# Top-k attention and two feed-forward blocks: a planner that begins score blocks and value blocks later than their inputs allow

## The chip, the cores and the metric

One core of a Trainium2 chip runs the whole program. The metric is the device time of one execution in microseconds (us); the kernel before takes 1037.14 us (median of 3 runs, 1036.56 to 1039.12). The engines are named as in the profile: PE (TensorE, matmuls; PEld its weight loads), DVE (VectorE), ACT (ScalarE), POOL (GpSimd) and SP, which issues the DMAs. Each engine works through a list of its own, one instruction after the other, and waits on semaphores for the others.

## The reference

Three stages, with 4 batches, 8 heads, 576 positions and head size 64, so 2304 rows of 512 values:

```python
scores = scale * np.matmul(q, k.transpose(0, 1, 3, 2))
kth = np.partition(scores, -top_k, axis=-1)[..., -top_k:-top_k + 1]   # top_k = 32
scores = np.where(scores >= kth, scores, -1000000000.0)
attn = np.exp(scores - np.max(scores, axis=-1, keepdims=True))
attn = attn / (np.sum(attn, axis=-1, keepdims=True) + 1e-09)
x = np.matmul(attn, v)                       # to 2304 x 512
h = x @ w_in
x = np.where(h > 0.0, h, np.exp(np.minimum(h, 0.0)) - 1.0) @ w_out
out = ((x @ w1) * (x @ w2)) @ w3 @ w_out2    # w_in 512x2048, w1 and w2 512x1024
```

## The kernel before, in words

**Tiles.** The 2304 rows are cut into 9 chunks of 256 rows, numbered 0 to 8. A chunk's attention is 8 tiles: 4 pairs of heads times 2 blocks of 128 rows. Its feed-forward part (function `mlp`) follows when the last tile is done. Most products are made from a high and a low half in 16 bits, so one product is three matmuls.

**One tile of attention**, in the order of its data:

- *Score block* (L529, PE): 4 matmuls `psS<-kt,qh` and `psS<-kt,ql` for one of the two heads. There is one `psS`, so the next score block can only start when ACT has copied this one into `s` (L531).
- *Top-k* (DVE): per head four MAX8 (L539) and three MATCH_REPLACE8 (L541) over 576 scores, in `wk`.
- *Weights*: ACT makes the mask and the exponential (L554, L556) and the high half (L564), POOL the low half (L565), and SP issues one transposing DMA per head, `pt<-pi` (L567).
- *Value block* (L582, PE): 28 matmuls `psA<-vv,pt`. There is one `psA` too; ACT reads the denominators from it (L593), DVE inverts and scales (L596, L599), ACT and POOL split the result (L602, L603), and SP issues `x<-xt` (L604), which makes a part of the chunk's `x`.

**The feed-forward part of a chunk** on PE: 16 A blocks (L841 to L843, `psR<-x,win`), 16 O blocks (L878 to L880, `psY<-g,wout`), two small gram products on the result (Y: L898, L903), 16 B blocks (L920 to L922, `psR<-x,w`), 12 matmuls each, and 8 D blocks (L955 to L957) of 6. A blocks read `x` of all eight tiles. Between A and O stand ACT and POOL (L853 to L865), in Y DVE (L891, L902, L904), between B and D ACT, DVE and POOL (L930 to L946).

**The weights** come as 64-bit numbers and are turned into scaled 16-bit halves in the first 250 us (L633 to L679, L783), while the first chunks' attention already runs.

**What sets the order.** No scheduler of the language: `Program.op` records every piece of work with an engine, an assumed cost, its inputs and outputs and a rank. `emit` then plans a timetable by list scheduling (`forward`, `backward`, then `forward` again, `fb=2` times): an operation becomes ready when its inputs have ended, plus an assumed latency (table `LAT`, times `slack` between engines), and an engine takes the ready one with the best rank. The instructions are written in the order of the planned starts. So a planned time decides only the order; on the chip nothing waits for it, only for semaphores. The table `OFF` (some 240 numbers, one for each group of work and engine) shifts the ranks of the first pass.

Of the kernel before, what the change touches and what calls it, by code (L numbers as in the profile page):

```python
# [32 lines left out]
PAR = dict(rings=(2, 3, 4, 3, 1, 2, 5, 3), nxs=3, nxf=2, nxt=3, slack=1.6, fb=2, snake=1, blag=0, hv={}, lv={'wi': 16, 'wo': 16}, whole=(), cd={'wi': [0, 0, 6], 'wo': [0, 0, 6], 'w34': [0, 0, 8], 'w12': [8, 0, 8]}, pv=-577.81, pi=702.591, p34=-453.754, po=123.714, p12=822.408,   # L33
# [5 lines left out]
OFF = {":DVE": 16163, "A0:ACT": -38685, "A0:DVE": -4543, "A0:PE": 21441, "A0:POOL": 23849, "A1:ACT": 1589, "A1:PE": -13628, "A1:POOL": -11110,  # L39
# [35 lines left out]
       "att8x:SP": 2116, "attsa:ACT": -38945, "attsa:PE": -45630, "attsk:ACT": -46655, "attsk:POOL": -12175, "attsk:SP": -20106, "attsm:ACT": 59355,  # L75
       "attsm:POOL": 27934, "attsp:ACT": -27773, "attsp:POOL": 4475, "attsp:SP": 12804, "attsq:ACT": -29254, "attsq:POOL": 26261, "attsq:SP": -8330,
       "attss:ACT": -10714, "attss:PE": -9165, "attst:DVE": 53351, "attsv:ACT": 18840, "attsv:DVE": 15311, "attsv:SP": 12330, "attsx:ACT": 11365,
# [3 lines left out]
       -8612, "w_in.c:ACT": 800, "w_in.c:DVE": 9028, "w_in.c:PE": -11799, "w_in.c:POOL": -7583, "w_in.n:DVE": 24888, "w_in.n:PE": 9694, "w_in:ACT":  # L81
       -220, "w_in:DVE": -7426, "w_in:POOL": -33659, "w_in:SP": -55119, "w_out.c:ACT": 5219, "w_out.c:DVE": -531, "w_out.c:PE": -22400,
       "w_out.c:POOL": -5233, "w_out.n:DVE": -38749, "w_out.n:PE": 8892, "w_out:ACT": 14086, "w_out:DVE": 35892, "w_out:POOL": 23776, "w_out:SP":
       23054, "w_v0:DVE": -70692, "w_v0:PE": -2179, "w_v0:SP": -19017, "w_v1:DVE": -12335, "w_v1:PE": 38647, "w_v1:SP": 59851, "w_v:DVE": -36828}


# [17 lines left out]
class Program:  # L104
# [30 lines left out]
    def forward(self, succ, rank):  # L135
# [6 lines left out]
        rt = [0.0] * n  # L142
# [949 lines left out]
```

## Time and profile before

| what | us |
|---|---|
| median of 3 runs | 1037.14 |
| the profiled execution, its own time | 1037.07 |
| its span, first to last instruction | 1035.3 |
| PE busy | 955.4 (92%) |
| DVE busy | 870.8 (84%) |
| ACT busy | 819.4 (79%) |
| POOL busy | 739.7 (71%) |

A page of the profile has a sum for each engine, which hides when it was busy. The stretches have to be read apart: in some of them one engine is full, and only work on that engine's list, or a wait in it, moves the end. Times in the profile count from the start of the span.

### The profile page before, as it was taken

The numbers are of one execution on the slowest core, as the hardware profiler recorded it, in microseconds if no ns is written. First come the engines' busy times: TensorE is split into PE (matmuls) and PEld (weight loads), VectorE is DVE, ScalarE is ACT, GpSimd is POOL, SyncE is SP. The second block draws the span as 40 slices with busy tenths as digits, with TensorE's granted clock in tenths as the row PEclk, the third lists the DMA queues.
The fourth block names the chain that finished last, engine by engine and source line by source line (L and its number), as shares of the span: only waits on it lengthen the run. The fifth ranks groups of instructions, "written<-read, shape, count | busy, mean of one in ns | idle before, by whom it ended". The sixth has DMA issues, their size and how long they took to land.

```text
span 1035.3 us, 24518 instructions
## 1 busy us (share of the span) xinstructions
PE 955.4 (92%) x9096; PEld 770.4 (74%) x9096; DVE 870.8 (84%) x1941; ACT 819.4 (79%) x1517; POOL 739.7 (71%) x795
## 2 busy tenths in 40 slices
PE   2466999896899999999999999999999999999998
PEld 2333455796788878878878897788789889878875
DVE  6999999999999999997999999575999999951010
ACT  6999977998999977976987798587778878944512
POOL 6999966799999846965985597479368657944701
PEclk9897999999999999999999999999999999999999
DMA  9987995867456774555476354524553353330000
GB/s 366 329 273 232 276 251 122 232 197 154 135 126 160 169 137 86 121 136 148 127 175 155 86 121 116 146 57 136 124 132 69 70 114 82 57 91 14 1 22 21
DMA packets 246744, 144.04 MB, mean 139 GB/s; under 512 B 195680, under 2 KB 222304, under 8 KB 246624
## 3 DMA queue, kind: packets, MB, share of 16 engines
q1 hardware_dynamic: 246624, 142.48, 54.1%
q8 instruction: 71, 1.16, 0.5%
q14 instruction: 49, 0.40, 0.1%
HBM read 80.65 MB, written 14.59 MB: 92 GB/s over the span
## 4 chain that ended last, share of the span: by engine, by line
DVE 36%; PE 26%; ACT 15%; POOL 7%; issue 7%; DMA 6%; DVEq 0%; POOLq 0%; ACTq 0%
DVE m L539 16%; DVE wk L541 14%; PE psY L783 3%; PE psR L920 2%; PE psR L921 2%; PE psR L922 2%; DMA pt<-pi 2%; PE psS L529 2%; DMA pp<-w 2%; PE psA L582 2%; ACT s L554 1%; PE psR L841 1%; PE psR L842 1%; PE psR L843 1%; ACT s L531 1%
## 5 line engine op out<-in xcount | busy, mean ns | idle before, releaser
L539 DVE MAX8 m<-wk 128x8 f32<-128x576 f32 x432 | 312.2, 747 | 0.8
L565 POOL TENSOR_TENSOR pi<-s,pi 128x576 f16<-128x576 f32 x144 | 185.5, 1296 | 78.8 <-ACT pi L564 67.7
L541 DVE MATCH_REPLACE8 wk<-m,wk 128x576 f32<-128x576 f32 x288 | 212.5, 741 | 0.0
L920 PE MATMUL psR<-x,w 128*128 128x256 f16 x576 | 157.3, 273 | 3.7 <-DVE t L940 3.7
L841 PE MATMUL psR<-x,win 128*128 128x256 f16 x576 | 157.8, 274 | 0.8 <-DVE t L940 0.5
L843 PE MATMUL psR<-x,win 128*128 128x256 f16 x576 | 157.4, 273 | 0.0
L842 PE MATMUL psR<-x,win 128*128 128x256 f16 x576 | 157.4, 273 | 0.0
L922 PE MATMUL psR<-x,w 128*128 128x256 f16 x576 | 157.0, 273 | 0.5 <-POOL w L670 0.5
L878 PE MATMUL psY<-g,wout 128*128 128x256 f16 x576 | 157.3, 273 | 0.0
L880 PE MATMUL psY<-g,wout 128*128 128x256 f16 x576 | 157.0, 273 | 0.0
L879 PE MATMUL psY<-g,wout 128*128 128x256 f16 x576 | 157.0, 273 | 0.0
L921 PE MATMUL psR<-x,w 128*128 128x256 f16 x576 | 157.0, 273 | 0.0
L554 ACT ACTIVATE s<-s,m 128x576 f32<-128x576 f32 x144 | 110.3, 776 | 40.8 <-DVE m L539 39.2
L529 PE MATMUL psS<-kt,qh 128*128 128x288 f32 x320 | 112.4, 366 | 31.4 <-ACT s L531 24.9
L531 ACT ACTIVATE s<-psS 128x576 f32<-128x576 f32 (+1 forms) x160 | 103.1, 644 | 17.0 <-PE psS L529 11.2
L556 ACT ACTIVATE s<-s,ty 128x576 f32<-128x576 f32 x144 | 107.4, 771 | 3.8 <-POOL ty L550 3.7
L539 DVE MAX8 m<-s 128x8 f32<-128x576 f32 x144 | 106.1, 746 | 3.9 <-ACT s L531 3.4
L541 DVE MATCH_REPLACE8 wk<-m,s 128x576 f32<-128x576 f32 x144 | 106.3, 741 | 0.0
L564 ACT ACTIVATE pi<-s 128x576 f16<-128x576 f32 x144 | 96.5, 679 | 9.4 <-DMA pt<-pi 9.1
L529 PEld LDWEIGHTS psS<-kt,qh 128*128 128x128 f32 x320 | 62.3, 195 | 44.9 <-ACT s L531 20.0
L529 PE MATMUL psS<-kt,ql 128*128 128x288 f32 x320 | 91.5, 300 | 1.0 <-POOL ql L511 1.0
L582 PEld LDWEIGHTS <-pt 128*128 128x128 f16 (+1 forms) x2240 | 77.8, 101 | 17.7 <-issue 8.0
(168 smaller groups left out, 2393.4 us busy)
## 6 DMA issues: line engine op xcount, KB each, us to landing
qr<-qd SPq DMA_DIRECT2D x72, 128.0 KB, 2.7
raw<-kd SPq DMA_DIRECT2D x32, 288.0 KB, 3.3
w<-w_in SPq DMA_DIRECT2D x16, 512.0 KB, 7.5
w<-w_out SPq DMA_DIRECT2D x16, 512.0 KB, 6.0
w<-w3t SPq DMA_DIRECT2D x16, 512.0 KB, 4.8
kd<-kt SPq DMA_DIRECT2D x12, 576.0 KB, 4.0
kt<-kd SPq DMA_DIRECT2D x12, 576.0 KB, 3.9
w<-w SPq DMA_DIRECT2D x12, 512.0 KB, 4.7
```

Source lines behind the costliest of these rows:

```text
L529: T.matmul(psS[:, half, 0:288], lhsT=L[qs][:, hh], rhs=KT[kk][:, hh, half * 288:half * 288 + 288], start=li == 0, stop=li == 1)
L539: op("DVE", 665, lambda r=r, src=src, m8=m8, hh=hh: V.max(m8[:, hh, 8 * r:8 * r + 8], src), [skey], [mk], p1 + PAR["ot"] * STEP)
L541: op("DVE", 727, lambda r=r, src=src, w=w, m8=m8, hh=hh: V.match_replace(w, m8[:, hh, 8 * r:8 * r + 8], src, -3.0e38), [skey, mk], [k], p1 ...
L565: op("POOL", 1240, lambda Y=Y, PIs=PIs, hh=hh: G.tensor_tensor(PIs[:, hh, S:2 * S], Y[:, hh], PIs[:, hh, 0:S], op=OP.subtract), hks, [pk], ...
L841: T.matmul(o, lhsT=hi(W)[:, cs], rhs=X[:, 0, kd_, 0:N], start=kd_ == 0, stop=False)
L842: T.matmul(o, lhsT=hi(W)[:, cs], rhs=X[:, 1, kd_, 0:N], start=False, stop=False)
L843: T.matmul(o, lhsT=lo(W)[:, cs], rhs=X[:, 0, kd_, 0:N], start=False, stop=kd_ == 3)
L878: T.matmul(o, lhsT=hi(W)[:, cs], rhs=rh, start=ft == 0 and m % 2 == 0, stop=False, skip_group_check=True)
L879: T.matmul(o, lhsT=hi(W)[:, cs], rhs=rl, start=False, stop=False, skip_group_check=True)
L920: T.matmul(o, lhsT=hi(W)[:, cs], rhs=X[:, 0, kd_, 0:N], start=kd_ == 0, stop=False)
L921: T.matmul(o, lhsT=hi(W)[:, cs], rhs=X[:, 1, kd_, 0:N], start=False, stop=False)
L922: T.matmul(o, lhsT=lo(W)[:, cs], rhs=X[:, 0, kd_, 0:N], start=False, stop=kd_ == 3)
```

## The change

`Program.op` takes one more argument, `late`; `forward` adds it to the time at which an operation becomes ready. The score blocks and the value blocks get 700 ns, nothing else does. The table `OFF` has new numbers in all its entries (one line of each side stands here for it). Every recorded operation, its inputs and its outputs are the same.

```diff
-PAR = dict(rings=(2, 3, 4, 3, 1, 2, 5, 3), ...
+PAR = dict(wq=700.0, wa=700.0, rings=(2, 3, 4, 3, 1, 2, 5, 3), ...
-OFF = {":DVE": 16163, "A0:ACT": -38685, "A0:DVE": -4543, "A0:PE": 21441, ...
+OFF = {":DVE": 14772, "A0:ACT": -36506, "A0:DVE": -3954, "A0:PE": 23705, ...
...
-    def op(self, eng, cost, fn, r=(), w=(), pr=0.0, lat=None, lk=False):
+    def op(self, eng, cost, fn, r=(), w=(), pr=0.0, lat=None, lk=False, late=0.0):
         i = len(self.ops)
+        if late:
+            self.late[i] = late
...
             for s in succ[i]:
-                rt[s] = max(rt[s], end + (0.0 if e == "SP" else LAT.get(...) * ...))
+                rt[s] = max(rt[s], end + (0.0 if e == "SP" else LAT.get(...) * ...) + self.late.get(s, 0.0))
...
-                        op("PE", 540, qk, [("qh", qs), ("ql", qs), ("k", kk)], ["psS"], pqk)
+                        op("PE", 540, qk, [("qh", qs), ("ql", qs), ("k", kk)], ["psS"], pqk, late=PAR["wq"])
...
-                    op("PE", 930, av, [("v", vs), ("vl", vs), ("pt", pt, 0), ("pt", pt, 1)], [pak], p5)
+                    op("PE", 930, av, [("v", vs), ("vl", vs), ("pt", pt, 0), ("pt", pt, 1)], [pak], p5, late=PAR["wa"])
```

Lines of the changed kernel are numbered 3 higher than those of before (L582 is L585, L593 is L596, and so on).

The lists move everywhere by a few places. Three places matter for what follows.

PE, chunk 6, the last value block (`pt1`, 64 columns: this tile's rows belong to two batches), the score blocks behind it, the next value block (`pt0`) and the chunk's first A block (`x0,win`). Before:

```order
L582 MATMUL psA_153<-vv3_115,pt1_123 64x64
L920 LDWEIGHTS w12_99
...
L529 MATMUL psS_152<-kt2_111,qh0_105 128x288
...
L920 MATMUL psR0_156<-x2_126,w12_99 128x256
...
L529 MATMUL psS_152<-kt2_111,qh1_106 128x288
...
L582 MATMUL psA_153<-vv3_115,pt0_122 128x65
...
L841 MATMUL psR1_157<-x0_124,win_97 128x256
```

After, the same stretch of PE's list:

```order
L585 MATMUL psA_153<-vv3_115,pt1_123 64x64
L532 MATMUL psS_152<-kt2_111,qh0_105 128x288
L532 MATMUL psS_152<-kt2_111,ql0_107 128x288
...
L532 MATMUL psS_152<-kt2_111,qh1_106 128x288
L532 MATMUL psS_152<-kt2_111,ql1_108 128x288
...
L585 MATMUL psA_153<-vv3_115,pt0_122 128x65
...
L844 MATMUL psR1_157<-x0_124,win_97 128x256
```

Before, six B blocks (L920 to L922) stand between that value block and the A block, two ahead of each of three score blocks; after, the three score blocks follow each other, and no B block is left between.

ACT, the last two value blocks of the program (L593, after L596, reads the denominators of each), with B's copies (L930, L939; after L933, L942) and D's (L962; after L965). Before:

```order
L593 ACTIVATE ty2_150<-psA_153 128x2
L602 ACTIVATE xt1_136<-xf0_138 128x128
L939 ACTIVATE t1_128<-psR0_156,sc_96 128x256
L945 ACTIVATE pp_140<-t1_128 128x2x256
L962 ACTIVATE t4_131<-psR1_157,sc_96 128x512
L930 ACTIVATE t3_130<-psR0_156,sc_96 128x512
L939 ACTIVATE t2_129<-psR1_157,sc_96 128x256
L939 ACTIVATE t2_129<-psR2_158,sc_96 128x256
L593 ACTIVATE ty3_151<-psA_153 128x2
```

After:

```order
L596 ACTIVATE ty2_150<-psA_153 128x2
L605 ACTIVATE xt1_136<-xf0_138 128x128
L933 ACTIVATE t0_127<-psR2_158,sc_96 128x512
L596 ACTIVATE ty3_151<-psA_153 128x2
L605 ACTIVATE xt2_137<-xf1_139 128x128
L965 ACTIVATE t3_130<-psR0_156,sc_96 128x512
L965 ACTIVATE t4_131<-psR1_157,sc_96 128x512
L942 ACTIVATE t2_129<-psR1_157,sc_96 128x256
```

The last value block has moved ahead of most of chunk 7's B blocks and of the last D blocks of chunk 6.

PE at the start of chunk 2, two score blocks (`kt0`, then `kt2`) that follow each other before:

```order
L394 MATMUL psR0_156<-pp_140 128x128
L529 MATMUL psS_152<-kt0_109,qh0_105 128x288
L529 MATMUL psS_152<-kt0_109,ql0_107 128x288
...
L529 MATMUL psS_152<-kt2_111,qh0_105 128x288
L529 MATMUL psS_152<-kt2_111,ql0_107 128x288
```

After, the same two score blocks:

```order
L532 MATMUL psS_152<-kt0_109,ql0_107 128x288
L585 LDWEIGHTS pt1_123
L585 MATMUL psA_153<-vv1_113,pt1_123 128x65
...
L901 MATMUL psY0_154<-x0_124 128x128
L402 MATMUL psR1_157<-ident_95,sc_96 128x128
L532 MATMUL psS_152<-kt2_111,qh0_105 128x288
L532 MATMUL psS_152<-kt2_111,ql0_107 128x288
...
L906 MATMUL psY0_154<-ident_95,ac0_141 128x128
L532 MATMUL psS_152<-kt0_109,qh0_105 128x288
```

A value block and the gram product of chunk 0's Y (L901) now stand between these two; the third score block has moved up, with one small product (L906) ahead of it. Over the whole list there are 159 gaps between score blocks. By the trace's durations of the work that stands in them, 57 held less than 2.7 us of PE work before (two blocks of 12 matmuls or less), 55 held 2.7 to 4.5 us and 47 more; after it is 28, 92 and 39.

## Rows read from the trace of the kernel before

**Rows 1.** Stretches: length; busy PE, PEld, DVE, ACT, POOL; clock, DMA share, GB/s

```profile
0.00:103.60 103.60, 55.30 (x309) 32.78 (x310) 91.01 (x186) 93.33 (x163) 91.02 (x90) 0.88 0.87 300
103.60:246.00 142.40, 132.82 (x1029) 92.15 (x1028) 138.92 (x310) 126.02 (x236) 113.67 (x120) 0.98 0.87 216
246.00:286.00 40.00, 29.14 (x327) 25.25 (x326) 38.48 (x90) 37.65 (x70) 39.58 (x43) 0.96 0.45 116
286.00:720.30 434.30, 427.14 (x4436) 363.24 (x4437) 395.42 (x892) 361.90 (x682) 323.94 (x355) 1.00 0.56 131
720.30:938.40 218.10, 217.87 (x2222) 182.64 (x2220) 198.80 (x446) 166.00 (x313) 137.17 (x158) 1.00 0.40 90
938.40:1035.30 96.90, 93.13 (x784) 74.30 (x781) 8.20 (x21) 34.53 (x59) 34.36 (x34) 1.00 0.04 13
```

**Rows 2.** PE's waits from 246 to 300 us, then from 300: total, times, longest

```profile
PE psS L529 <- ACT s L531: 7.5, 5, 2.8
PE psR L920 <- DVE t L940: 2.6, 2, 1.3
...
PE psS L529 <- ACT s L531: 2.6, 4, 1.1
PE psY L898 <- DVE x L891: 1.3, 3, 0.6
PE psR L920 <- DVE t L940: 1.1, 1, 1.1
PE psA L582 <- DMA pt<-pi: 0.5, 1, 0.5
```

**Rows 3.** Timeline of PE: start, us, instruction, idle before; two adjoining score blocks

```profile
246.38 0.29 PE L529 MATMUL psS<-kt,ql 128*128 128x288 f32 x1
249.32 0.40 PE L529 MATMUL psS<-kt,qh 128*128 128x288 f32 x1 [2.64 <-ACT s L531]
```

**Rows 4.** Timelines of PE and SP: end of chunk 6's attention, its first A block

```profile
759.72 0.66 PE L582 MATMUL psA<-vv,pt 128*64 128x65 f16 x15
...
771.02 1.02 PE L582 MATMUL psA<-vv,pt 128*128 128x65 f16 x28
771.88 0.27 PE L841 MATMUL psR<-x,win 128*128 128x256 f16 x1
...
767.73 1.20 SPq L604 DMA_TRANSPOSE x<-xt  x1
```

**Rows 5.** Transposing DMAs of L604, then L567: issues, landing times

```profile
L604 SPq DMA_TRANSPOSE x<-xt x72: 1167/1170/3114, 124.6 to 941.9; - x72
DMA to landing us min/median/max: 2.3/2.4/5.1
...
L567 SPq DMA_TRANSPOSE pt<-pi x144: 1242/1301/3794, 33.1 to 923.2; - x144
DMA to landing us min/median/max: 2.8/3.0/7.5
```

**Rows 6.** Timelines of PE and DVE: a late score block of chunk 6, its first top-k

```profile
720.30 0.38 PE L529 MATMUL psS<-kt,qh 128*128 128x288 f32 x1
720.92 0.28 PE L878 MATMUL psY<-g,wout 128*128 128x256 f16 x1
...
722.64 0.75 DVE L539 MAX8 m<-s 128x8 f32<-128x576 f32 x1
```

**Rows 7.** Timelines of DVE, PE, SP: the last top-k, the last value block

```profile
915.59 1.39 DVE L891 SCALAR_TENSOR_TENSOR x<-psY,sc,x 128x512 f16<-128x512 f32 x2
916.90 0.75 DVE L539 MAX8 m<-wk 128x8 f32<-128x576 f32 x1
...
937.08 0.27 PE L920 MATMUL psR<-x,w 128*128 128x256 f16 x1
938.39 1.01 PE L582 MATMUL psA<-vv,pt 128*128 128x65 f16 x28
939.24 0.27 PE L920 MATMUL psR<-x,w 128*128 128x256 f16 x1
...
941.89 1.17 SPq L604 DMA_TRANSPOSE x<-xt  x1
```

**Rows 8.** Timeline of PE, a D block: three matmuls from one to the next

```profile
912.12 0.38 PE L955 MATMUL psR<-w,pp 128*128 128x512 f16 x1
912.77 0.38 PE L955 MATMUL psR<-w,pp 128*128 128x512 f16 x1
```

**Rows 9.** DVE from that first top-k to the last, columns as in rows 1

```profile
722.60:917.60 195.00, 194.77 (x2001) 164.62 (x1999) 193.49 (x430) 155.62 (x294) 128.85 (x148) 1.00 0.42 94
```

**Rows 10.** The stretch around the wait of rows 3, columns as in rows 1

```profile
244.00:252.00 8.00, 5.20 (x51) 4.55 (x49) 8.00 (x16) 7.97 (x16) 8.00 (x9) 0.88 0.47 111
```

More of the change, by code (lines that the diff above doesn't have):

```diff
@@ L31 @@
 FLAT = 2.0 ** -100
-PAR = dict(rings=(2, 3, 4, 3, 1, 2, 5, 3), nxs=3, nxf=2, nxt=3, slack=1.6, fb=2, snake=1, blag=0, hv={}, lv={'wi': 16, 'wo': 16}, whole=(), cd={'wi': [0, 0, 6], 'wo': [0, 0, 6], 'w34': [0, 0, 8], 'w12': [8, 0, 8]}, pv=-577.81, pi=702.591, p34=-453.754, po=123.714, p12=822.408,
+PAR = dict(wq=700.0, wa=700.0, rings=(2, 3, 4, 3, 1, 2, 5, 3), nxs=3, nxf=2, nxt=3, slack=1.6, fb=2, snake=1, blag=0, hv={}, lv={'wi': 16, 'wo': 16}, whole=(), cd={'wi': [0, 0, 6], 'wo': [0, 0, 6], 'w34': [0, 0, 8], 'w12': [8, 0, 8]}, pv=-577.81, pi=702.591, p34=-453.754, po=123.714, p12=822.408,
            pis=-107.607, pos=19.797, p12s=-197.302, p34s=838.328, ci=825.351, co=-921.962, cos=928.659, c12=388.003, m34=497.922, c34=2463.442,
@@ L37 @@
            pvb=-3829.627, lag1=-475.176, lagb=401.111)
-OFF = {":DVE": 16163, "A0:ACT": -38685, "A0:DVE": -4543, "A0:PE": 21441, "A0:POOL": 23849, "A1:ACT": 1589, "A1:PE": -13628, "A1:POOL": -11110,
[35 rows of a table removed]
-       "att8x:SP": 2116, "attsa:ACT": -38945, "attsa:PE": -45630, "attsk:ACT": -46655, "attsk:POOL": -12175, "attsk:SP": -20106, "attsm:ACT": 59355,
-       "attsm:POOL": 27934, "attsp:ACT": -27773, "attsp:POOL": 4475, "attsp:SP": 12804, "attsq:ACT": -29254, "attsq:POOL": 26261, "attsq:SP": -8330,
-       "attss:ACT": -10714, "attss:PE": -9165, "attst:DVE": 53351, "attsv:ACT": 18840, "attsv:DVE": 15311, "attsv:SP": 12330, "attsx:ACT": 11365,
[3 rows of a table removed]
[L81 to L84, printed above, removed]
+OFF = {":DVE": 14772, "A0:ACT": -36506, "A0:DVE": -3954, "A0:PE": 23705, "A0:POOL": 13235, "A1:ACT": 9762, "A1:PE": 885, "A1:POOL": -2900, "A2:ACT":
[35 rows of a table added]
+       -38671, "attsa:PE": -34217, "attsk:ACT": -47585, "attsk:POOL": -18790, "attsk:SP": -24324, "attsm:ACT": 80164, "attsm:POOL": 42349,
+       "attsp:ACT": -14019, "attsp:POOL": 1784, "attsp:SP": 2858, "attsq:ACT": -27343, "attsq:POOL": 29970, "attsq:SP": -8355, "attss:ACT": -5402,
+       "attss:PE": -2050, "attst:DVE": 62681, "attsv:ACT": 8171, "attsv:DVE": 4178, "attsv:SP": 3805, "attsx:ACT": 8137, "attsx:DVE": -58648,
[3 rows of a table added]
+       "w_in.c:DVE": 15806, "w_in.c:PE": -13574, "w_in.c:POOL": -2986, "w_in.n:DVE": 24902, "w_in.n:PE": 10368, "w_in:ACT": 5488, "w_in:DVE": -6693,
+       "w_in:POOL": -26382, "w_in:SP": -50075, "w_out.c:ACT": 4587, "w_out.c:DVE": 2699, "w_out.c:PE": -24388, "w_out.c:POOL": -5784, "w_out.n:DVE":
+       -45892, "w_out.n:PE": 4020, "w_out:ACT": 17362, "w_out:DVE": 34891, "w_out:POOL": 27794, "w_out:SP": 32129, "w_v0:DVE": -67268, "w_v0:PE": -83,
+       "w_v0:SP": -9652, "w_v1:DVE": -7227, "w_v1:PE": 32560, "w_v1:SP": 60807, "w_v:DVE": -30407}
 def conv_modes(n, d, g, s=0):
@@ L113, in __init__ @@
         self.readers = {}
-    def op(self, eng, cost, fn, r=(), w=(), pr=0.0, lat=None, lk=False):
+        self.late = {}
+    def op(self, eng, cost, fn, r=(), w=(), pr=0.0, lat=None, lk=False, late=0.0):
         i = len(self.ops)
+        if late:
+            self.late[i] = late
         deps = set()
@@ L185, in forward @@
             for s in succ[i]:
-                rt[s] = max(rt[s], end + (0.0 if e == "SP" else LAT.get((eng, self.ops[s][0]), 130.0) * (1.0 if eng == self.ops[s][0] else PAR["slack"])))
+                rt[s] = max(rt[s], end + (0.0 if e == "SP" else LAT.get((eng, self.ops[s][0]), 130.0) * (1.0 if eng == self.ops[s][0] else PAR["slack"])) + self.late.get(s, 0.0))
                 miss[s] -= 1
```

76 rows, old and new, of the table OFF are left out of this document.

## The prediction, made before the changed kernel was run

> **What bounds the kernel now.** The page's busy shares were read first: PE 92%, DVE 84%, ACT 79%, POOL 71%, near enough to each other that no sum decides. Next the stretches [rows 1]. Up to 286 us PE is idle for 48.3 + 9.6 + 10.9 = 68.8 us, while DVE, ACT and POOL are busy for 80 to 99% of each part of it: the vector engines, which prepare the weights and the first chunks, set the pace. From 286 to 938.4 us PE is busy for 427.1 + 217.9 of 652.4 us: its own list is the bound, and DVE has some 58 us to spare. The last 97 us are PE alone. So after 286 us the time moves only with what PE waits for. Third, PE's waits [rows 2]: from 300 us on they are a few us in all, 2.6 of them at score blocks and 0.5 at value blocks. Fourth, the timelines around the places where the lists show large moves; they come below.
>
> **What the change can give.** It puts more work between the scores and their successors, so that PE waits less for `psS`. From 300 us on, the waits of the kinds that it addresses are 2.6 + 0.5 = 3.1 us [rows 2]; all of PE's idle time from 286 to 938.4 us is 7.4 us [rows 1]. From 246 to 300 us scores wait 7.5 us, for 2.64 us where two blocks adjoin [rows 2, 3]. The new list separates those two and brings the third closer instead. I count nothing for this stretch: DVE, ACT and POOL are busy 38.5, 37.7 and 39.6 of its 40 us [rows 1], and what PE does there (weight norms, B blocks of chunk 0, then A of chunk 1) waits for their results, as the 2.6 us at L920 show. If that cover were absent, the whole idle time of 10.9 us could go. In the other direction, the lists of the vector engines shift by one to five us up to there, and a later weight could cost PE about 3 us. So the gain is 3.1 us, with bounds of -3 and 7.4 + 10.9 = 18.3.
>
> **What it moves, first place: chunk 6's A blocks.** Before, PE starts that chunk's last value block (two halves, for two batches) at 759.72, the last part of `x` is issued at 767.73 and can land 2.3 us later at the earliest, at 770.0; the A block starts at 771.88 [rows 4, 5]. So the chain from value block to `x` takes 10.3 us, and 12.2 us of PE work lie beside it: two halves of a value block, six B blocks, three score blocks and the next value block. After, the six B blocks are gone from there. A value block takes 0.85 us (938.39 to 939.24), a score block 0.62 (720.30 to 720.92) [rows 6, 7]; what is left is 2 x 0.85 + 3 x 0.62 + 0.85 = 4.4 us. PE then waits 10.3 - 4.4 = 5.9 us. The fastest such chain in the rows is the last one, 938.39 to 941.89 plus 2.3, 5.8 us with one half [rows 5, 7], which would leave 5.8 + 0.85 - 4.4 = 2.2 us. But the three score blocks now adjoin and share one `psS`: two waits of about 2.64 us [rows 3], 5.3 us, in the same stretch. I take 5.6, between 5.3 and 5.9.
>
> **Second place: the last value block.** In the list of before, PE has 218.1 us from the score block at 720.30 to the last value block at 938.39, all of it work [rows 1, 6, 7]. Counted in the two lists, that stretch held 32 A, 37 O, 42 B and 24 D blocks, 38 score and 20 value blocks; now it holds 32 A, 34 O, 34 B and 17 D blocks and as many of the others. Eighteen blocks have left it: eight B and four D stand behind the last value block now, three O and three D ahead of the score block. A block of 12 matmuls takes 1.31 us (937.08 to 938.39), a D block 2 x 0.65 = 1.30 us [rows 7, 8]. So 18 x 1.30 = 23.4 us less, and 194.7 us are left.
>
> Beside it runs a chain that does not get shorter. The score block's first top-k on DVE starts 2.3 us after it, at 722.64, and the last top-k ends at 916.90 + 0.75 = 917.65 [rows 6, 7]; between them DVE is busy 193.5 of 195.0 us [rows 9]. Only the two L891 and two small operations have left that stretch of DVE's list, 1.5 us, so 193.5 us stay. From the last top-k to the last issue of L567 at 923.2 it is 5.6 us, and 2.8 us more to the earliest landing [rows 5], 8.4 in all. 2.3 + 193.5 + 8.4 = 204.2 us. The last value block, with everything listed behind it on PE, waits 204.2 - 194.7 = 9.5 us. Below: if DVE's remaining idle time of 1.5 us goes, and PE starts with the head that landed first, some 0.4 us earlier, 7.6 us. Above: an L567 landing of 4.3 us, between the usual 3.0 and the longest 7.5, makes it 11 us. I take 8.5, between 7.6 and 9.5.
>
> The first place lies inside this stretch, so the two are not added: 194.7 + 5.6 = 200.3 us of PE is still shorter than the chain. If the chain should be quicker than I reckon, 5.3 us of loss stay from the first place. The Y products of chunk 6 and the B blocks of that chunk wait for DVE work in the same lagging list; those waits are parts of the same 8.5 us, taken earlier.
>
> **The clock.** After PE's wait of 2.64 us the stretch 244 to 252 had a granted clock of 0.88 [rows 10], a part of it at the lower of the two levels (1.2 of 2.4 GHz); that is 0.12 x 8 = 1.0 us. Before, all stretches from 286 us on have 1.00 [rows 1]. One wait of several us near the end should cost this once: 1.0 us, bounds 0 and 2 (it may fall twice).
>
> The Trainium skill, page "TensorE: Matmul & The Clock Gate", section "What's actually happening", says that the throttled state is the default and that only activity lifts it. By that rule each of the two places costs one such fall, 2 us rather than 1, and the forecast would be 1 us later; the 0.88 of [rows 10] agrees.
>
> **Does anything pass a waiting matmul?** In [rows 3] PE stands idle for 2.64 us, and nothing listed behind the waiting block starts. So I count PE's waits in full, with the B and D blocks behind them. The same page, section "Step-by-step: what each phase is for", says that matmuls stay in program order and only weight loads are pulled ahead. If matmuls could pass, the 8.5 us would vanish and 1034 us be left; the trace agrees with the rule.
>
> **The sum.** The profiled execution took 1037.07 us (span 1035.3 and 1.8 around it), the median of the runs is 1037.14. 1037.1 + 8.5 + 1.0 - 3.1 = 1043.5; I say 1043.
>
> **The rivals.**
>
> *Faster: PE reaches the score block of 720 us earlier.* Both the list and the chain of the second place start at this score block, so whatever PE gains ahead of it is kept in full. For it: 10.9 + 7.2 us of idle time lie between 246 and 720 us, most of it at score blocks or right beside them. Against it: the full vector engines there. If 7 of the 10.9 and 6 of the 7.2 us go, it is 1037.1 + 8.5 + 1 - 13 = 1033.6. It wins from a gain of 12.7 us. Chance 0.16.
>
> *No change.* The chain is 8.5 us too long by my reckoning in part: the top-k of the late tiles no longer waits for scores, which are now up to 13 us ahead of it, and the chain loses 2 to 3 us, down to the first place's 5.3; the gain ahead is 5 us. 1037.1 + 5.3 + 0.5 - 5 = 1037.9. Chance 0.20.
>
> *Much slower: waits that feed each other.* DVE, ACT and POOL also work their lists in order, and near the end many of their instructions wait for PE (denominators, Y, B). A PE that waits for DVE may make DVE wait for PE. With the upper bounds, 11 + 2 and no gain, plus one more wait of 2.64 us: 1037.1 + 15.6 = 1052.7. Against it: DVE has scores waiting all the time there. Chance 0.06.
>
> *The change does nothing to the order* is excluded: more than a third of the operations stand elsewhere in their engine's list.
>
> **How the numbers follow.** A measurement of this kernel can tell about 0.3%, 3.1 us, from no change: faster is under 1034.0, slower over 1040.2. The forecast, a loss of 3.1 to 13 us, has 0.58: with the smallest terms (7.6 + 0) it holds up to a gain of 4.5 us, with the largest (11 + 2) and no gain it ends at 1050. With the last rival, slower has 0.64, no change 0.20, faster 0.16. The range of 1034 to 1050 leaves out most of the faster rival and the feeding waits, 2 in 10. The likeliest case alone runs from 1040.2 to 1050.
>
> **What will show it.** Right: PE's waits after 720 us, 0.2 us now, are 5 us or more, with waits at A (for `x<-xt`), at adjoining score blocks near 770 us, and at value blocks or Y behind DVE near 835 to 935 us; the last value block starts about 930 to 935 instead of 938.4, with 93.1 + 12 x 1.30 = 108.7 us of PE work behind it instead of 93.1; waits of L529 from 300 to 720 us fall below 1 us; a slice near the end has a granted clock below 1.00. Wrong: PE idle for under 3 us between 720 us and the last value block, or PE's idle time up to 286 us smaller than 69 us by 8 or more.

## The result, and the profile after

The changed kernel takes 1047.01 us (median of 4 runs, 1046.56 to 1047.93), the kernel before beside it on the same chip 1038.13 us (1036.56 to 1039.99). The ratio is 1.0079, 95% interval 1.0056 to 1.0103: slower, by 8.9 us. The forecast was 1043 us, between 1034 and 1050. The profiled execution is the longest of the four, 1047.93 us with a span of 1046.2; before it was 1037.07 and 1035.3.

The six stretches after, cut at the times of [rows 1] and with their columns (the last one ends at the new end):

```profile
0.00:103.60 103.60, 51.98 (x302) 31.94 (x302) 86.58 (x178) 88.22 (x153) 87.09 (x87) 0.85 0.90 296
103.60:246.00 142.40, 130.60 (x989) 87.61 (x990) 140.43 (x310) 129.25 (x242) 113.05 (x118) 0.99 0.84 204
246.00:286.00 40.00, 31.69 (x307) 26.82 (x305) 38.31 (x85) 34.41 (x63) 39.40 (x42) 0.91 0.51 136
286.00:720.30 434.30, 425.61 (x4428) 361.17 (x4427) 396.42 (x891) 360.75 (x677) 320.49 (x352) 1.00 0.56 130
720.30:938.40 218.10, 214.02 (x2235) 181.95 (x2233) 203.80 (x460) 170.25 (x322) 144.23 (x165) 0.99 0.43 96
938.40:1046.20 107.80, 103.99 (x846) 82.23 (x843) 8.61 (x21) 37.57 (x63) 35.83 (x35) 1.00 0.04 16
```

PE's idle time (length less PE's busy time) has become 51.6, 11.8, 8.3, 8.7, 4.1 and 3.8 us; it was 48.3, 9.6, 10.9, 7.2, 0.2 and 3.8. So some is lost in nearly every stretch, and the largest single piece, 3.9 us, after 720 us. The 40 us from 246 on, where the list separates the two score blocks of [rows 3], have gained 2.6 us.

PE's waits after (total, times, longest), first from 246 to 300 us, then from 300 us on, as [rows 2]:

```profile
PE psR L923 <- DVE t L943: 2.3, 1, 2.3
...
PE psS L532 <- ACT s L534: 1.0, 3, 0.5
...
PE psA L585 <- DVE xf L602: 3.2, 4, 1.2
PE psY L901 <- DVE x L894: 2.7, 2, 1.7
PE psS L532 <- ACT s L534: 2.2, 3, 1.0
PE psR L923 <- DVE t L943: 1.7, 2, 1.0
```

From 246 to 300 us the waits for scores fell from 7.5 to 1.0 us. From 300 us on they are 2.2 us against 2.6. In their place stand waits of value blocks for DVE (3.2 us) and of Y for DVE (2.7 against 1.3).

The first place (timeline of PE, with SP's issue of the last part of `x`), which answers to [rows 3, 4]:

```profile
771.83 1.07 PE L585 MATMUL psA<-vv,pt 128*64 128x65 f16 x28
772.83 0.28 PE L923 MATMUL psR<-x,w 128*128 128x256 f16 x1
...
774.25 1.08 PE L585 MATMUL psA<-vv,pt 128*64 128x65 f16 x28
775.25 0.40 PE L532 MATMUL psS<-kt,qh 128*128 128x288 f32 x1
776.79 0.40 PE L532 MATMUL psS<-kt,qh 128*128 128x288 f32 x1 [0.74 <-ACT s L534]
778.60 0.40 PE L532 MATMUL psS<-kt,qh 128*128 128x288 f32 x1 [1.01 <-ACT s L534]
780.54 0.95 PE L585 MATMUL psA<-vv,pt 128*128 128x65 f16 x14 [0.61 <-DMA pt<-pi]
781.30 0.40 PE L844 MATMUL psR<-x,win 128*128 128x256 f16 x1
...
783.43 0.27 PE L844 MATMUL psR<-x,win 128*128 128x256 f16 x1
...
778.53 1.55 SPq L607 DMA_TRANSPOSE x<-xt  x1
```

From that issue to its landing, in the trace of after:

```profile
DMA to landing us min/median/max: 2.7/2.7/2.7
```

The three score blocks adjoin, and two of them wait for the copy of the one before, 0.74 and 1.01 us. One B block (L923 to L925) still stands between the two halves of the last value block. From the first matmul of the first A block to that of the second it is 2.13 us instead of the 1.31 of a block at full clock.

The second place (timelines of PE and DVE), which answers to [rows 6, 7]:

```profile
733.11 0.38 PE L532 MATMUL psS<-kt,qh 128*128 128x288 f32 x1
734.72 0.75 DVE L542 MAX8 m<-s 128x8 f32<-128x576 f32 x1
...
922.40 1.42 DVE L542 MAX8 m<-wk 128x8 f32<-128x576 f32 x2
933.59 1.01 PE L585 MATMUL psA<-vv,pt 128*128 128x65 f16 x28
```

The score block that stood at 720.30 starts at 733.11, and the last value block at 933.59 follows without a wait. Five windows, as [rows 9, 10] and for the first place:

```profile
734.70:923.80 189.10, 185.02 (x1941) 158.81 (x1940) 189.03 (x427) 154.41 (x292) 127.92 (x147) 0.99 0.44 97
244.00:252.00 8.00, 8.00 (x89) 7.25 (x88) 8.00 (x23) 7.10 (x13) 7.81 (x9) 1.00 0.70 192
770.00:794.00 24.00, 21.64 (x252) 18.70 (x250) 24.00 (x55) 20.79 (x42) 14.87 (x18) 0.93 0.52 114
776.00:779.50 3.50, 1.75 (x18) 1.40 (x18) 3.50 (x10) 1.80 (x4) 1.36 (x3) 1.00 1.24 170
779.60:782.90 3.30, 2.69 (x30) 2.10 (x27) 3.30 (x8) 3.08 (x5) 0.20 (x1) 0.50 0.27 62
```

DVE is busy for 189.03 of 189.10 us between its first and its last top-k there. The stretch around 246 us has full clock now, the one around the first place 0.93: the clock is at half from 779.6 to 782.9 us, behind the waits of 0.74 and 1.01 us and ahead of the one of 0.61.

**One measure for all kernels.** The lists differ, so the same time on the clock means different work. I take a block's start less the durations of all work listed ahead of it on PE, each piece with its duration in the execution of before. This "lost time" counts idle time and half clock alike; only its differences matter, and a few tenths of a us mean nothing. It is worked out from the PE timelines of the profiled executions, for three blocks: the first A block of chunk 1, the score block of [rows 6], and the last value block.

| profiled execution | first A of chunk 1 | score block | last value block |
|---|---|---|---|
| before | 65.7 | 71.8 | 72.0 |
| after | 69.6 | 77.0 | 82.9 |
| e1, lateness alone | 77.2 | 82.8 | 88.6 |
| e2, table alone | 68.9 | 82.5 | 89.5 |
| e3, start of before | 66.4 | 73.9 | 79.8 |
| e4, start of after | 73.8 | 79.6 | 79.6 |
| e5, end of after | 67.5 | 73.5 | 79.5 |
| e6, end of before | 66.0 | 82.5 | 82.4 |
| e7, loads behind w_in | 64.9 | 73.4 | 79.8 |
| e8, middle of after | 66.4 | 83.2 | 83.1 |
| e9, blocks back | 69.9 | 77.9 | 95.3 |
| e10, short top-k in after | 70.9 | 78.3 | 80.9 |
| e11, the same in 16 tiles | 67.8 | 75.5 | 80.7 |
| e12, short top-k in before | 69.4 | 75.0 | 74.3 |

After less before is 3.9, then 1.3 more, then 5.7 more: 10.9 us, the difference of the two spans.

### The profile page after: what moved, and what is told of

It reads as the page before. It is cut to its first block, busy times and chain, and to the rows that moved or that the text cites. A ratio compares the mean times of both kernels' runs of the same rounds, so it can differ in the third digit from the quotient of the medians.

```text
span 1046.2 us, 24494 instructions
## 1 busy us (share of the span) xinstructions
PE 957.9 (92%) x9096; PEld 771.7 (74%) x9096; DVE 874.2 (84%) x1941; ACT 820.5 (78%) x1517; POOL 740.1 (71%) x795
## 4 chain that ended last, share of the span: by engine, by line
PE 44%; DVE 28%; ACT 11%; DMA 5%; POOL 4%; issue 4%; SPq 0%; DVEq 0%; ACTq 0%; POOLq 0%
DVE m L542 12%; DVE wk L544 10%; PE psR L844 3%; PE psR L845 3%; PE psR L846 3%; PE psS L532 3%; PE psY L881 3%; PE psY L882 3%; PE psY L883 3%; PE psA L585 3%; PE psR L923 3%; PE psR L924 3%; PE psR L925 3%; PE psY L786 2%; DMA pt<-pi 2%
## 5 line engine op out<-in xcount | busy, mean ns | idle before, releaser
L923 PE MATMUL psR<-x,w 128*128 128x256 f16 x576 | 158.3, 275 | 4.5 <-DVE t L943 4.0
L925 PE MATMUL psR<-x,w 128*128 128x256 f16 x576 | 158.0, 274 | 0.0
L557 ACT ACTIVATE s<-s,m 128x576 f32<-128x576 f32 x144 | 109.3, 774 | 54.6 <-DVE m L542 53.6
L532 PE MATMUL psS<-kt,qh 128*128 128x288 f32 x320 | 112.5, 366 | 22.8 <-ACT s L534 15.6
L542 DVE MAX8 m<-s 128x8 f32<-128x576 f32 x144 | 105.3, 747 | 12.7 <-ACT s L534 12.5
L567 ACT ACTIVATE pi<-s 128x576 f16<-128x576 f32 x144 | 95.2, 678 | 7.5 <-DMA pt<-pi 7.2
L532 PE MATMUL psS<-kt,ql 128*128 128x288 f32 x320 | 92.3, 302 | 0.0
L866 POOL TENSOR_TENSOR t<-t,t 128x512 f32<-128x512 f32 x68 | 88.6, 1304 | 3.3 <-ACT t L865 1.4
L532 PEld LDWEIGHTS psS<-kt,qh 128*128 128x128 f32 x320 | 63.1, 197 | 37.0 <-ACT s L534 13.3
```

The lines of the kernel that those rows point to most:

```text
L532: T.matmul(psS[:, half, 0:288], lhsT=L[qs][:, hh], rhs=KT[kk][:, hh, half * 288:half * 288 + 288], start=li == 0, stop=li == 1)
L542: op("DVE", 665, lambda r=r, src=src, m8=m8, hh=hh: V.max(m8[:, hh, 8 * r:8 * r + 8], src), [skey], [mk], p1 + PAR["ot"] * STEP)
L923: T.matmul(o, lhsT=hi(W)[:, cs], rhs=X[:, 0, kd_, 0:N], start=kd_ == 0, stop=False)
L925: T.matmul(o, lhsT=lo(W)[:, cs], rhs=X[:, 0, kd_, 0:N], start=False, stop=kd_ == 3)
```

## The experiments

All medians are compared with before's on the same chip: 1039.67 us beside e1 to e4, 1039.34 beside e5 to e8, 1037.99 beside e9 to e12. e1 to e6 and e8 change only which plan the operations are listed by; their lines (and e7's and e9's) are numbered higher, e1 to e6 and e8 by 67 against after.

**e1 and e2: one part of the change alone.** e1 has the old table and the lateness, e2 the new table without it.

```diff
 e1: OFF as in before, wq=700.0, wa=700.0
 e2: OFF as in after,  wq=0.0,   wa=0.0
```

Expected of e1:

> The table OFF of before with the 700 ns of the change. Theory 'places' (the loss comes from three places of the lists: the loads at the start, chunk 6's A blocks, the last value blocks): here 218 us of PE work stay between the late score block and the last value block, as before, and 8.6 us (before 11.3, after 3.7) between chunk 6's last value block and its first A block, so about 1037 to 1041. Rival 'lateness' (700 ns on score and value blocks make the list worse as such): 1044 to 1048, as after.

Expected of e2:

> The table OFF of after without the 700 ns. Theory 'places': the SP list of the start is that of after (about +3 us), the stretch to the last value block is 199.7 us (after 194.6), chunk 6's A blocks have 26 us of cover; about 1041 to 1045. Rival 'lateness': about 1038, as before. A third, 'mismatch' (a table found with the lateness does badly without it, and the other way round): both this one and the late-only kernel are slower than after.

Measured: e1 1053.64 us, ratio 1.0131 (1.0114 to 1.0148); e2 1055.08 us, 1.0151 (1.0132 to 1.0170). e1 lies over both of its theories; e2 came as its third one, 'mismatch'. Either part alone is worse than both. A table belongs to the rule that it was set for: neither number can be read as the price of "the lateness", and the loss of after is not the sum of two parts. What e1 and e2 lose their time on is not worked out here beyond the table.

**e3 and e4: the start exchanged.** The plan of one list up to 110 us of its planned times, then the other's for what is not placed yet.

```diff
 e3: up to 110 us as before, then as after
 e4: up to 110 us as after, then as before
```

> The plan of before up to 110 us of planned time, then the plan of after. Theory 'places' puts about 3 us of the loss into the first 110 us (PE's idle time up to the first L783 is 51.8 after and 48.7 before): 1043 to 1044.5. Rival 'all behind 720 us': no change from after, 1046 to 1047.5.

> The plan of after up to 110 us, then that of before. Theory 'places': about 3 us over before, 1040.5 to 1042. Rival 'all behind 720 us': as before, 1037 to 1038.5. If idle time of the start is hidden later, also as before.

Measured: e3 1044.64 us, ratio 1.0045 (1.0030 to 1.0060); e4 1045.86 us, 1.0056 (1.0041 to 1.0071). By the times alone, the start costs something in both: e3, by the ratios 0.34% or 3.5 us under after, is near 'places', and e4 lies over both theories. By the table, e4 loses 8.1 us more than before up to the first A of chunk 1, more than after does (3.9): the seam at 110 us probably costs something of its own. But from the score block on e4, with before's end, loses 0.0 us, and e3, with after's end, 5.9.

**e5, e6 and e8: the end and the middle exchanged.**

```diff
 e5: up to 640 us as before, then as after
 e6: up to 640 us as after, then as before
 e8: up to 110 us as before, up to 640 us as after, then as before
```

> The plan of before up to 640 us of its planned times, then the plan of after: three adjoining score blocks in chunk 6, 3.7 us of PE work as cover for its A blocks, 194.6 us of PE work from the score block of the second place to the last value block. Theory 'places' (the end of the list costs PE's waits there): 5 to 7 us over before, PE's waits from 720 us on 3.5 to 6 us. Rival 'start only' (all of the loss is from the first 110 us): as before within 1.5 us.

> The plan of after up to 640 us of its planned times, then the plan of before: 11.3 us of cover for chunk 6's A blocks, 217.9 us of PE work to the last value block. 'Places': 3 to 5 us over before (what the start costs, and no more), PE's waits from 720 us on under 1.5 us. Rival 'start only': 7 to 9 us over before, as after.

> The plan of before up to 110 us, of after from 110 to 640 us, of before again to the end. 'Places' (the middle is neither gain nor loss): within 2 us of before. Rival 'the lateness pays in the middle and start and end take it back': 3 us or more under before.

Measured: e5 1045.11 us, ratio 1.0054 (1.0034 to 1.0074); e6 1048.22 us, 1.0086 (1.0068 to 1.0105); e8 1048.67 us, 1.0085 (1.0069 to 1.0102). e5's time came as 'places' has it, 5.8 us over before; its waits from 720 us on are 2.6 us, less than the 3.5 named, and half clock makes up the rest. e6's time is where 'start only' has it, 8.9 us over before, but the start is not the reason: e8, with before's start, takes as long and misses both of its theories. The windows of e6 show why (640 to 720 us, and from there to 938.4, columns as in rows 1):

```profile
640.00:720.00 80.00, 72.71 (x767) 62.94 (x765) 52.09 (x118) 56.53 (x106) 48.00 (x53) 0.96 0.39 100
720.00:938.40 218.40, 218.19 (x2236) 184.34 (x2234) 205.18 (x457) 173.24 (x324) 145.50 (x166) 1.00 0.43 96
```

PE idles 7.3 us just behind the seam, which neither list does there (0.7 us in before, 1.7 in after). e6's waits in those 80 us:

```profile
PE psS L599 <- ACT s L601: 4.9, 2, 3.2
PE psY L968 <- DVE x L961: 2.4, 1, 2.4
```

Behind it, with before's end, 0.2 us of idle time are left in 218.4. The same windows of e5 (640 to 720, 720 to 790, 790 to 930) have it the other way round:

```profile
640.00:720.00 80.00, 79.40 (x800) 65.62 (x798) 46.67 (x102) 54.23 (x99) 48.34 (x53) 1.00 0.44 97
720.00:790.00 70.00, 67.57 (x671) 56.57 (x670) 67.49 (x151) 53.79 (x101) 38.95 (x45) 0.95 0.55 127
790.00:930.00 140.00, 139.78 (x1464) 119.75 (x1461) 134.04 (x308) 114.55 (x218) 101.64 (x117) 1.00 0.39 84
```

So a splice's total is no measure of the part exchanged; what holds is the stretch away from the seam. Between score block and last value block, after's end loses 5.9, 5.9, 6.0 and 6.4 us (after, e3, e5, e7), before's end 0.2, 0.0, -0.1 and -0.1 (before, e4, e6, e8). The end's loss is the list's there, whatever ran ahead of it. In e5 it falls before 790 us: 2.43 us of idle time, and 0.05 x 70 = 3.5 us lost to half clock.

**e7: SP's order at the start.** In after, two loads of v (`raw<-vd`) and one store of k's halves (`kd<-kt`) stand ahead of the last load of `w_in` on SP's list.

```diff
-SP: raw<-vd, a load, raw<-vd, nine loads, w_in, kd<-kt, w_in, w_out
+SP: a load, nine loads, w_in, w_in, raw<-vd, raw<-vd, kd<-kt, w_out
```

> The lists of after, with three DMAs of its start on SP's list (two loads of v, one store of k's halves) put behind the last load of w_in, where the list of before has them. Theory 'SP's order costs the start': last w_in issue near 23 us instead of 26.8, first product with prepared weights 2 to 4 us earlier than 111.3 us, time 2 to 4 us under after. Rival (the later score blocks of the first chunk's second tile, or the weight norms, cost it): within 1 us of after.

Measured: 1046.28 us, ratio 1.0070 (1.0049 to 1.0092); after had 1.0079. Timeline of SP in e7:

```profile
20.44 5.55 SPq L424 DMA_DIRECT2D w<-w_in  x2
26.04 0.90 SPq L424 DMA_DIRECT2D raw<-vd  x2
```

The two last loads of `w_in` together end at 25.99; the last was expected near 23 and was issued at 26.75 in after. SP holds the second back for some 5 us although nothing is listed between them. The first product with prepared weights starts at 109.56 us instead of 111.26, 1.7 us earlier where 2 to 4 were expected. The time is within 1 us of after, as the rival has it. That speaks against SP's order of these three as the cause, but the two intervals overlap so far that some 2 us are not excluded. The lower lost time of its execution (64.9) is within what equal lists show: e6 and after have the same list up to 640 us, and 66.0 against 69.6.

**e9: the six B blocks put back.** A piece of PE's list is rewritten (S a score block, V a value block); as a consequence one mask on ACT (L557) changes places with the copy of a B block, and the other lists stay.

```diff
-PE: B B S B B B S B B S V(half) B V(half) S S S V A A
+PE: B S B S V(half) V(half) B B S B B S B B S V A S A
```

> The lists of after with one local edit on PE: the last two halves of chunk 6's value blocks move ahead of six B blocks, and the score blocks behind them are set between those, two B blocks ahead of each, as in before. 11.3 us of PE work instead of 3.7 lie between that value block and chunk 6's first A block; 194.6 us to the last value block stay. Theory 'first place by itself' (the adjoining score blocks and the short cover cost the end's time): 4 to 6 us under after, so 2 to 4 over before, PE's waits from 720 us on under 1.5 us. Theory 'DVE's chain' (the prediction: DVE is full up to the last top-k, and PE waits for it somewhere): PE now waits ahead of the value block that was moved up or of a later one; 0 to 2 us under after, waits from 720 us on still 4 to 6 us.

Measured: 1059.92 us (1054.34 to 1060.83), ratio 1.0190 (1.0160 to 1.0220): some 12 us over after, far outside both theories. Timelines of PE and ACT in e9 (L1028 is the copy of a B block, L942 in after):

```profile
768.55 0.66 PE L671 MATMUL psA<-vv,pt 128*64 128x65 f16 x14 [0.68 <-DMA pt<-pi]
772.71 2.32 PE L671 MATMUL psA<-vv,pt 128*64 128x65 f16 x42 [3.49 <-DMA pt<-pi]
779.27 0.40 PE L618 MATMUL psS<-kt,qh 128*128 128x288 f32 x1 [1.10 <-ACT s L620]
...
778.20 0.47 ACT L1028 ACTIVATE t<-psR,sc 128x256 f32<-128x256 f32 x1 [10.45 <-PE psR L1011]
```

PE comes to the value block too early and waits for `pt`, 0.68 and 3.49 us. The B blocks stand behind it, so ACT waits 10.45 us for the first of them, and ACT's later work, copies of scores among it, stands behind that. From the score block to the last value block 17.4 us are lost, against 5.9 in after. The run doesn't tell the theories apart. It shows that this way of filling the gap from PE's list alone fails.

**e10, e11 and e12: less work for DVE near the end.** The last round of top-k (one MATCH_REPLACE8 and one MAX8 of each head) is left out, from the score block of 733 us on.

```diff
+short = r == 3 and idx >= 108          # e11: 112; r == 2 for the MATCH_REPLACE8
-V.max(m8[...], src)
+None if short else V.max(m8[...], src)
-th = m8[:, :, 31:32]
+th = (m8[:, :, 23:24] if idx >= 108 else m8[:, :, 31:32])
```

> The lists of after, but from the score blocks of 733 us on (18 tiles) top-k stops one round earlier: it leaves out the last MATCH_REPLACE8 and MAX8 of each head, so the threshold is the 24th score there. Takes 36 times some 1.4 us, about 50 us, off DVE. 'DVE's chain': the end's whole loss goes, 5 to 7 us under after, PE's waits from 720 us on under 1 us. 'First place by itself': the adjoining score blocks still wait for their copies, 1.7 us and their half clock stay, 3 us or less under after.

> As the kernel with 18 shortened tiles, but only the 16 tiles of chunks 7 and 8 are shortened (leaving out the same two operations of each head there); the tiles on which chunk 6's A blocks wait keep their whole top-k. 'DVE's chain' as the prediction puts it (the wait of the last value block decides, the first place only lies inside it): chunk 6's A blocks still cost their 4 to 5 us, so 0 to 2 us under after. 'DVE's chain to chunk 7's value blocks alone': 4 us or more under after.

> The lists of before with the same 18 tiles shortened as in after's version, leaving out the last round of their top-k. Control: PE's list is the bound of before's end, with 0.2 us of waits from 720 us on, so within 1.5 us of before by every theory. If it is 3 us or more under before, DVE also sets the end of before, and the comparison of the two lists was read wrongly.

Measured: e10 1044.08 us, ratio 1.0050 (1.0030 to 1.0070); e11 1043.75 us, 1.0051 (1.0030 to 1.0072); e12 1038.45 us, 0.9989 (0.9968 to 1.0010). By the ratios e10 is 0.29% and e11 0.28% under after, some 3 us, and the intervals overlap. For e10 that is what 'first place by itself' has, at its edge; for e11 it lies between both theories. The windows say more. e10, from 720.3 to 790 us and on to 938.4, and then e11:

```profile
720.30:790.00 69.70, 66.77 (x684) 55.81 (x683) 57.18 (x124) 53.12 (x101) 40.26 (x46) 1.00 0.54 134
790.00:938.40 148.40, 148.40 (x1565) 126.48 (x1565) 99.50 (x230) 119.10 (x226) 104.89 (x122) 1.00 0.38 80
```

```profile
720.30:790.00 69.70, 67.37 (x667) 56.08 (x664) 63.72 (x138) 51.64 (x98) 38.22 (x43) 0.95 0.54 129
790.00:938.40 148.40, 148.40 (x1565) 126.39 (x1563) 98.09 (x226) 118.87 (x225) 104.15 (x121) 1.00 0.39 80
```

e10's waits of PE from 720.3 us on (the value block is L586 there):

```profile
PE psS L532 <- ACT s L534: 1.7, 3, 0.8
PE psA L586 <- DMA pt<-pi: 1.0, 1, 1.0
PE psS L532 <- DMA kt<-kd: 0.2, 1, 0.2
```

With DVE busy for 57.18 instead of some 66 of these 69.7 us, and for 99.5 of the next 148.4, the 2.9 us of idle time at the first place stay in e10, at the adjoining score blocks and at the value block behind them. What goes are the waits after 790 us, 148.40 - 146.68 = 1.7 us in the execution of after, and in e10 the half clock. So most of the end's loss stands at the first place: in after, 2.4 us of waits and up to 1.7 us of half clock, of 5.9. No run parts the adjoining score blocks without moving something else, so what each of the waits there costs is read from the trace and not from an experiment. e12 came as expected: DVE does not set the end of before.

No version beats both kernels, and none of these pieces points to one: no stretch of after is shown to gain on before.

## Why the prediction was right

The direction and the size held: 8.9 us of loss, 6.4 forecast (1043.5 from 1037.1). The sum came near by luck, from two errors of opposite sign. For the end (second place and clock) 9.5 us were forecast and 5.7 measured; ahead of it a gain of 3.1 us was forecast and a loss of 5.2 measured. These are the two profiled executions, whose spans differ by 10.9 us, 2 us more than the medians.

**The gain ahead of the score block: 3.1 us forecast, a loss measured.** The waits that the change addresses did fall: at score blocks from 246 to 300 us by 6.5 us, and from 300 to 720 us to less than 1 us, as forecast (0.5 us from 286 to 720.3). But PE's total did not. From the first A of chunk 1 to the score block, before's plan loses 6.1, 6.0 and 5.6 us (before, e5, e12), after's 7.4, 7.5, 8.5 and 8.0 (after, e3, e7, e9): 1.3 to 2.4 us more than in before. The step "the waits of these kinds go, 3.1 us" took waits away and put none in their place. From 286 to 720.3 us PE's waits for DVE rose from 2.7 to 7.5 us, while those for scores and for `pt` fell from 4.0 to 0.5. The largest of them after:

```profile
PE psA L585 <- DVE xf L602: 2.8, 3, 1.2
PE psY L901 <- DVE x L894: 1.7, 1, 1.7
PE psR L923 <- DVE t L943: 1.7, 2, 1.0
...
PE psS L532 <- ACT s L534: 0.5, 1, 0.5
```

For 246 to 286 us the cover named, the full vector engines, was there: 6.5 us of waits less, 2.6 us of idle time less.

**The start, counted at nothing with bounds of -3 and 10.9.** Up to the first A of chunk 1 after's list loses 69.6, 66.0, 69.9, 70.9 and 67.8 us (after, e6, e9 to e11; mean 68.8), the kernels with before's start 65.7, 66.4, 67.5, 66.4 and 69.4 (before, e3, e5, e8, e12; mean 67.1): some 1.7 us, within the bounds and smaller than what one list varies from run to run. The times disagree: e3, with before's start, is some 3.5 us under after, but e6 and e8, which differ only in the start, are within 0.5 us of each other. That the start costs after something is likely, not shown; what in it would cost is open, and e7 speaks against three DMAs of SP.

**The second place, 8.5 us: the step that failed most.** The prediction let the chain of 204.2 us decide against 194.7 us of PE work. The work came as counted. The chain measured 1.6 us from the score block to the first top-k (2.3 forecast), 189.1 us of top-k (193.5; the idle time of DVE in [rows 9] went, as in the lower bound, and some of DVE's list with it), and then at least 8.4: 199.1 us. PE needed 200.5, because it had already lost time, most of it at the first place; the last value block does not wait. The prediction had named this case ("5.3 us of loss stay from the first place") but summed up without it: the path that it took as the longer one was 5 us shorter than forecast. e10 and e11 fit that: with 47 and 43 us less work on DVE in all, the end still loses 2.6 and 5.2 us, against 5.9 in after. The chain is not far behind, though: with 194.7 us of PE work and no loss at the first place, the last value block would have waited some 4.4 us for it (an estimate, 199.1 - 194.7).

**The first place, 5.6 us, "not added": most of the end's loss.** From the value block of 771.8 us to that of chunk 7's third tile, 4.4 us are lost in after, 6.6, 6.1 and 7.3 in e3, e5 and e7. Both of its reckonings of the price were too simple. The adjoining score blocks wait 0.74 and 1.01 us, not twice 2.64: ACT, which copies them, is busy 20.79 of 24 us here and 7.97 of 8 at [rows 3, 10]. The chain to `x` took 9.4 us here, from 771.83 to its landing 2.7 us after 778.53, not 10.3; and beside it stood 5.7 us of PE work, not 4.4, since the prediction left out the B block between the two halves. With the waits ahead of it the A block, at 781.30, just finds `x`, landed at 781.2. So the short cover adds nothing to those waits, but without them PE would have stood at the A block for some of the same time (argued from these rows, not run). The rest is the wait for `pt` (0.61) and the clock.

**The clock: 1.0 us forecast, bounds 0 and 2.** A fall came, once, at the first place: 0.07 x 24 = 1.7 us in after, and 3.5 us in e5. The 1.0 us was read too small, because [rows 10] end inside the fall. In before the clock is at half up to 253.5 us:

```profile
250.00:254.00 4.00, 3.84 (x46) 3.73 (x46) 4.00 (x10) 3.93 (x7) 4.00 (x6) 0.57 0.51 122
```

That is 0.43 x 4 = 1.7 us, as in after. And it fell after shorter waits than the prediction asked for, 0.74 and 1.01 us instead of "several us". The Trainium skill, page "TensorE: Matmul & The Clock Gate", section "What's actually happening", says that how much of a kernel's first work meets the lower clock differs from run to run of one kernel. The granted 0.95 (e5, e11) and 1.00 (e10) from 720 to 790 us, with 2.3 to 2.9 us of idle time each, show something like it late in a kernel, though between kernels with nearly the same PE list there and not between runs of one.

**Does anything pass a waiting matmul?** Nothing did: in e9 PE stands idle for 3.49 us at a value block while B blocks with all their inputs are listed behind it, and these keep ACT waiting. The mechanism of the rival "waits that feed each other" is real, then, but it took e9 to see it. In after DVE waits for PE once from 720 us to the last value block, 2.5 us, behind its last top-k.

**The rivals.** PE reached the score block 5.2 us later in lost time, not 12.7 earlier: the faster rival had its sign wrong; of the engines that the prediction named against it, DVE is the one that PE waited for from 286 us on. "No change" had the end nearly right (5.3 + 0.5 us against 5.7) but needed a gain of 5 us ahead. Had the forecast taken its end, it would have been 1039.8 with its own gain, further off.

**The marks named.** Held: the last value block at 933.6 us, with 108.8 us of PE work behind it; waits of L532 from 300 to 720 us under 1 us; a granted clock of 0.98 from 720.3 to 790 us. Not held: PE's idle time after 720 us is 4.1 us, between the 5 asked for and the 3 that would have refuted it, chunk 6's A blocks do not wait for `x`, and the waits after 790 us are 1.7 us, not the main part. PE's idle time up to 286 us, 71.7 us, did not come out smaller.

## What to carry to other kernels

When two engines are nearly full, count a gap only once, and count it where it comes first: a PE that has already waited early arrives late enough to find the later inputs ready, as at the last value block here. A wait removed by reordering is a gain only in part while the engine behind it is full (here 6.5 us of waits less gave 2.6 us); look at that engine's busy share in the same stretch before booking it. And do not price a part of a plan by splicing two plans: the seam of e6 had 7 us of waits of its own, and one engine's list rewritten alone cost 12 in e9; compare the stretches away from the seam.

## What the runs showed that was not expected

- The lower clock was granted in after behind waits of 0.74 and 1.01 us, in e11 behind 0.74 and 0.80 us, and not at all in e10, with 0.74, 0.80 and 0.96 us at the same place: 0 to 3.5 us for nearly the same waits.
- Two adjoining score blocks cost 0.74 and 1.01 us of waiting in after, where ACT had room (1.6 us at the longest, in e7), and 2.64 us in before, where ACT was full.
- Up to the first A of chunk 1, profiled executions with the same list up to there differ by 4.9 us (66.0 to 70.9, e6 and e10), more than the change moves there.
